# A recurrence in chunks of 32 tokens over all four batches instead of chunks of 64 over two, ahead of a mixture-of-experts attention and an MLP

## The chip, the core and the metric

One Trainium2 chip, one of its cores. The time is the device time in microseconds (us) of one launch. Three runs of the kernel before took 1216.72, 1219.43 and 1217.4 us, median 1217.4.

## What is computed

Three stages in float32. Batch B = 4, heads H = 8, sequence S = 768, head width D = 40. The first is a linear recurrence with a state of 40x40 for each batch and head:

```python
for t in range(S):
    y[:, :, t] = np.einsum('bhd,bhde->bhe', rt, state)
    Sa = np.einsum('bhde,bhe->bhd', state, at)
    state_decay = state * wt[:, :, None, :] - np.einsum('bhd,bhe->bhde', Sa, bt)
    state = state_decay + np.einsum('bhd,bhe->bhde', vt, kt)
```

Its output, 4x768x320, goes through causal attention with 4 experts (two are chosen for each token by a gate) and then through a gated MLP with a product over the sequence (768x768). The change touches the recurrence and what stands around it; attention and MLP keep their code.

## The kernel before

**The recurrence in chunks.** Within a chunk of tokens the recurrence becomes matrix products: a product with the state at the chunk's start, a triangular system that couples the chunk's tokens (its inverse is applied as a product), and the update of the state. The kernel before (`recurrence`, L55 to L509) has chunks of 64 tokens, two batches at a time, and goes through 24 steps (2 pairs of batches, 4 units of 3 chunks each).

**A step's chain** (`p2`). `f_w` (L370): right side of the system, from state and values. `f_u1` (L387): inverse of the first 32x32 block. `f_t21` (L397): the coupling of the two blocks. `f_u2` (L404): inverse of the second. `f_s` (L416): update of the state. Between two of them ScalarE copies PSUM to SBUF (L374, L391, L400), and after the last VectorE adds the old state and scales it (L419, L420). That makes five products one after the other. Between them the program puts the output of the step before (`rr`, `vt`, `amat`, `ys`, `yk`: L295, L302, L316, L333, L341) and, in `pump`, pieces of the preparation.

**The preparation** (`p1`, one unit at a time). Loads of w, b, k and a in pieces of 30 KB (L134) are transposed on TensorE (L141). VectorE forms cumulative products of w by scans (`p_w`, L159, L165) and scales the others (L171, L178). `p_t` (L189) makes the triangular blocks, masked into SBUF by L193. `p_l` (L217) turns them so that 96 blocks of 32x32 lie on 96 partitions, `p_sub` (L227, L229) inverts them by 31 pairs of VectorE instructions, and `p_xt` (L237) turns the inverses back; ScalarE copies each turn (L196, L197, L218, L241). There are 8 units.

**What sets the order.** TensorE's order is the program's (`manual_schedule`). The other engines' queues are ordered by the compiler's own timeline, so that VectorE's order is seen only in the program built.

**Around it.** While the last unit runs, `tail` already works on the attention of batch 0 in the gaps; the weights and the input of that attention are made ready before (`pre`: `attn_prep`, `first_x`). Afterwards `blend` interleaves four `attention(b)` (weight 58.0 each) with the preparation of the MLP (`rest`) and four `mlp(b)` (49.8 each).

Of the kernel before, what the change touches and what calls it, by code (L numbers as in the profile page):

```python
# [7 lines left out]
F32 = mybir.dt.float32  # L8
# [47 lines left out]
def recurrence(ctx, tc, r, k, v, w, a, b, ident, store_x, pre=None, tail=None):
    nc = tc.nc
    B, H, S, D = r.shape
    C = 64
    BQ = 2  # L60
    CQ = 3
    UC = BQ * CQ
    UT = UC * C
    NU = S // (CQ * C)
    NP = H // 2
    TS = 96
    SL = UT // TS
# [24 lines left out]
    WL = [home(i, 3).tile([128, H, UT], F32, name=f"WL{i}") for i in range(3)]
    KBT = [home(i, 3).tile([128, NP, UC, Q], F32, name=f"KBT{i}") for i in range(3)]
    XTD = cp.tile([128, 2, H, UC, 32], F32, name="XTD")
    XT = [XTD[:64, i] for i in range(2)]
    TD = XTD[64:96].rearrange("j x h c t -> j (x h c t)").rearrange("j (t g h c) -> j t g h c", t=32, g=2, h=H)
    T21 = [XTD[96:, i] for i in range(2)] + [ep.tile([128, H, UC, 32], F32, name="T21")[96:]]
    RT = [cp.tile([Q, NP, BQ * C], F32, name=f"RT{i}") for i in range(RTB)]
    PP = [home(i, PPB).tile([Q, NP, UC, C + 1], F32, name=f"PP{i}") for i in range(PPB)]
    PEN = [home(i, 3).tile([D, H, UC], F32, name=f"PEN{i}") for i in range(3)]  # L100
    W65 = [ap.tile([Q, UC * (C + 1) + 1], F32, name=f"W65{i}") for i in range(2)]
    RPE = [ap.tile([Q, UC, C + 1], F32, name=f"RPE{i}") for i in range(2)]
    ABD = [ap.tile([Q, UT], F32, name=f"ABD{i}") for i in range(2)]
    VU = [cp.tile([128, H, C], F32, name=f"VU{q}") for q in range(BQ)]
    SV = [[cp.tile([128, H, C], F32, name=f"SV{q}{i}") for i in range(2)] for q in range(BQ)]
    S0 = [[cp.tile([Q, NP, 64], F32, name=f"S0{q}{i}") for i in range(2)] for q in range(BQ)]
    HR = [slice(h * 64, h * 64 + D) for h in range(2)]

    nc.vector.memset(mask, 1.0)
    for h in range(2):  # L110
        nc.gpsimd.affine_select(mask[h * 64:(h + 1) * 64], mask[h * 64:(h + 1) * 64], pattern=[[1, C]],
                                compare_op=OP.is_gt, fill=0.0, base=0, channel_multiplier=-1)
    nc.vector.memset(scan1, 0.0)
    nc.vector.memset(scan1[:, :, 0:1], 1.0)
    for t in SLAB:
        nc.vector.memset(t[:, :, :, D:], 1.0)
    nc.vector.memset(RR[:, :, D:], 1.0)
    for t in W65:
        nc.vector.memset(t, 0.0)
    for t in WL + VU + sum(SV, []):  # L120
        nc.gpsimd.memset(t, 0.0)

    src = {"w": w, "k": k, "b": b, "a": a}
    uses = []

    def load(n):
        if n >= len(uses):
            return
        nm, i, p = uses[n]
        bb, u = units[i]  # L130
        for q in range(BQ):
            for z in range(SL // BQ):
                t0 = u * CQ * C + z * TS
                nc.sync.dma_start(SLAB[n % NSL][:, q * SL // BQ + z, :, :D],  # L134
                                  src[nm][bb * BQ + q, 2 * p:2 * p + 2, t0:t0 + TS, :].rearrange("h p d -> p h d"))

    def tr(nm, i, p):
        n = uses.index((nm, i, p))
        pt = ps.tile([128, SL, TS], F32, name="p1", bufs=P1B)
        for s in range(SL):  # L140
            nc.tensor.transpose(pt[:, s, :], SLAB[n % NSL][:, s].rearrange("p h d -> p (h d)"), ident[:TS, :TS])  # L141
        load(n + NSL)
        return pt[:Q].rearrange("e s p -> e (s p)")

    def ct(x):
        return x.rearrange("e (c t) -> e c t", c=UC)

# [1050 lines left out]
```

## Time and profile before

| | us |
|---|---|
| median of 3 runs | 1217.4 |
| span of the profiled execution (no other time is listed for it) | 1222.0 |
| TensorE busy / weight loads / VectorE / ScalarE / GpSimd | 1024.8 / 896.5 / 761.9 / 652.2 / 203.0 |
| first of the chain's products (L370) of the first step, last of the 24th | 100.1, 692.2 |
| last output product of the recurrence (L341) | 735.9 |

The profiled execution is 4.6 us (0.4%) above the median of the runs. Busy times of the engines overlap, so they are read by stretch and against what each waits for. In the trace a float32 matmul stands as two records (L370: 24 steps of 16 matmuls, 768 records); a transpose through TensorE is one record.

### The profile page before, as it was taken

To read this page: it belongs to the slowest core of one execution; us is meant where nothing else is said; L and a number is where in the kernel's file an instruction comes from. 1 tells how busy PE (TensorE), PEld (TensorE's weight loads), DVE (VectorE), ACT (ScalarE), POOL (GpSimd) and SP (SyncE) were. 2 spreads that over 40 slices of the span, in tenths; PEclk is the share of its full clock that TensorE was granted. 3 is DMA by queue.
4 is the path that set the end of the run, shared out by engine and by line. 5 is a ranking of instruction groups with operands and counts; after the bars stand their busy time and mean duration, and the time that the engine had idled before them with its cause. 6 is when DMAs were issued, how large, how long until landed. Compare 5 with 4: busy or idle time off the path is not lost.

```text
span 1222.0 us, 31926 instructions
## 1 busy us (share of the span) xinstructions
PE 1024.8 (84%) x12730; PEld 896.5 (73%) x12730; DVE 761.9 (62%) x1930; ACT 652.1 (53%) x1599; POOL 203.0 (17%) x381
## 2 busy tenths in 40 slices
PE   5757787787887969879797877798999899999998
PEld 3546676777776868768685665576898798789888
DVE  4586739467495474854835446988657656765650
ACT  2345564655645557465455445667555556555641
POOL 5011000010010100000002015802211211121131
PEclk9999767666766566676675766799999999989999
DMA  4333343333333333323211103210000001000000
GB/s 64 61 63 62 53 67 62 54 57 55 69 60 57 56 52 69 64 45 80 53 41 33 28 7 107 68 39 1 18 32 17 1 17 49 1 1 17 18 1 33
DMA packets 214663, 52.96 MB, mean 43 GB/s; under 512 B 204785, under 2 KB 210673, under 8 KB 214514
## 3 DMA queue, kind: packets, MB, share of 16 engines
q1 hardware_dynamic: 214514, 50.92, 21.2%
q8 instruction: 100, 1.64, 0.6%
q14 instruction: 49, 0.40, 0.1%
HBM read 39.07 MB, written 7.86 MB: 38 GB/s over the span
## 4 chain that ended last, share of the span: by engine, by line
PE 48%; DVE 28%; ACT 14%; issue 5%; DMA 3%; POOL 2%; SPq 1%; ACTq 0%; DVEq 0%; POOLq 0%
DVE X L229 5%; DVE sub L227 5%; PE mm L952 4%; PE mm L953 4%; PE mm L954 4%; ACT XTD L196 3%; ACT XTD L241 3%; PE p L141 2%; PE mp L911 2%; PE y L333 2%; PE mp L841 2%; PE pw L404 2%; PE y L341 2%; ACT f L881 2%; PE p L217 2%
## 5 line engine op out<-in xcount | busy, mean ns | idle before, releaser
L141 PE MATMUL p<-ident,slab 96*128 96x96 f32 x512 | 102.4, 340 | 43.7 <-ACT XTD L197 20.0
L141 PEld LDWEIGHTS p<-ident,slab 96*128 96x128 f32 x512 | 73.7, 194 | 60.7 <-ACT XTD L197 22.4
L227 DVE TENSOR_TENSOR sub<-L,X 96x31 f32<-96x31 f32 (+15 forms) x248 | 83.4, 336 | 17.0 <-ACT L L218 10.5
L196 ACT COPY XTD<-p 32x192 f32<-32x192 f32 x64 | 30.6, 479 | 110.4 <-DVE WL L193 109.9
L229 DVE TENSOR_TENSOR X<-X,sub 96x31 f32<-96x31 f32 (+15 forms) x248 | 83.1, 335 | 6.0
L881 ACT ACTIVATE f<-sc,nm 128x512 f32<-128x512 f32 (+2 forms) x110 | 59.4, 544 | 31.6 <-DVE nm L876 14.4
L602 DVE TENSOR_TENSOR ptl<-mp,pth 128x256 fp32r<-128x256 f32 (+2 forms) x126 | 57.0, 460 | 23.1 <-ACT pth L601 22.1
L876 DVE TENSOR_REDUCE nm<-sc 128x1 f32<-128x512 f32 (+2 forms) x110 | 54.6, 505 | 22.9 <-PE sc L874 18.6
L333 PE MATMUL y<-RT,S 40*40 40x64 f32 (+1 forms) x768 | 49.5, 308 | 22.4 <-DVE am L322 22.4
L159 DVE TENSOR_TENSOR_SCAN PP<-W,scan 104x390 f32<-104x390 f32 x32 | 30.9, 966 | 58.4 <-ACT W L157 58.4
L601 ACT CAST pth<-mp 128x256 fp32r<-128x256 f32 (+2 forms) x126 | 50.0, 409 | 32.3 <-PE mp L911 18.4
L202 POOL COPY PEN<-PP 40x6 f32<-40x6 f32 x64 | 25.7, 401 | 245.0 <-DVE PP L159 243.6
L333 PEld LDWEIGHTS y<-RT,S 40*40 40x40 f32 (+1 forms) x768 | 43.2, 194 | 25.6 <-DVE am L322 23.7
L193 DVE TENSOR_TENSOR WL<-p,mask 64x384 f32<-64x384 f32 x32 | 17.9, 560 | 67.6 <-PE xt L189 67.1
L316 PE MATMUL y<-RT,vut 40*64 40x64 f32 x1536 | 48.1, 259 | 12.2 <-ACT S L383 11.8
L911 PE MATMUL mp<-ident,f 128*128 128x128 f32 x294 | 51.5, 295 | 4.6 <-DVE f L897 2.3
L920 PE MATMUL pa<-pth,vv 128*128 128x256 f32 x168 | 47.5, 297 | 5.9 <-DVE at L932 3.8
L316 PEld LDWEIGHTS y<-RT,vut 40*64 40x64 f32 x1536 | 37.7, 164 | 19.0 <-ACT S L383 14.7
L952 PE MATMUL mm<-ws_h,vn_h 128*128 128x384 f32 x144 | 49.2, 341 | 0.4 <-ACT vn_h L601 0.3
L171 DVE TENSOR_TENSOR kb<-p,RPE 104x384 f32<-104x384 f32 x64 | 35.2, 554 | 22.4 <-PE p L141 20.9
L897 DVE TENSOR_SCALAR f<-f,sm 128x128 f32<-128x128 f32 (+2 forms) x96 | 45.3, 513 | 5.9 <-POOL sm L889 5.3
L953 PE MATMUL mm<-ws_l,vn_h 128*128 128x384 f32 x144 | 48.6, 338 | 0.0
(284 smaller groups left out, 3122.1 us busy)
## 6 DMA issues: line engine op xcount, KB each, us to landing
slab<-in_w_dram SPq DMA_DIRECT2D x128, 30.0 KB
slab<-in_b_dram SPq DMA_DIRECT2D x128, 30.0 KB
slab<-in_k_dram SPq DMA_DIRECT2D x128, 30.0 KB
slab<-in_a_dram SPq DMA_DIRECT2D x128, 30.0 KB
SV<-in_v_dram SPq DMA_DIRECT2D x48, 80.0 KB
VU<-in_v_dram SPq DMA_DIRECT2D x48, 80.0 KB
RR<-in_r_dram SPq DMA_DIRECT2D x48, 80.0 KB
WL<-ABD SPq DMA_DIRECT2D x64, 60.0 KB
```

Source lines behind the costliest of these rows:

```text
L141: nc.tensor.transpose(pt[:, s, :], SLAB[n % NSL][:, s].rearrange("p h d -> p (h d)"), ident[:TS, :TS])
L196: nc.scalar.copy(TD[:, :, g, n].rearrange("j t c -> j c t"), pt[gs, :, gs])
L227: nc.vector.tensor_mul(tv, L[:, j + 1:, j:j + 1].to_broadcast([96, n, m]), X[:, j:j + 1, :m].to_broadcast([96, n, m]))
L229: nc.vector.tensor_sub(X[:, j + 1:, :m], X[:, j + 1:, :m], tv)
L316: nc.tensor.matmul(pas[h][js, q, p], st["vut", q][HR[h], p, js], rt[q][HR[h], p], start=True, stop=True)
L333: nc.tensor.matmul(st["py"][q][hr.start:hr.start + m, p], s0[q][hr, p, :m], rt[q][hr, p], start=(p == 0), stop=False, skip_group_check=True)
L602: (lo_eng or nc.vector).tensor_sub(lo, src, hi.bitcast(F32))
L876: nc.vector.tensor_reduce(nm[:, z:z + 1], sc[:, :nn], op=OP.max, axis=AX.X, negate=True)
L881: nc.scalar.activation(pe[:, n0:n0 + nn], scs[z][:, :nn], AF.Exp, bias=nm[:, :1], accum_out=sm[:, z, i - i0:i - i0 + 1])
L911: nc.tensor.transpose(pp[:, j, z * 128:(z + 1) * 128], pes[z][:, (j0 + j) * 128:(j0 + j + 1) * 128], ident)
L952: nc.tensor.matmul(ps_, ah, bh, start=first, stop=False)
L953: nc.tensor.matmul(ps_, ah, bl_, start=False, stop=False)
```

## The change

The host lays w, k, b, a, r and v out anew (`layouts`): the 40 channels of a pair of batches on partitions 0 to 39 and 64 to 103, chunks of 32 tokens in 24 contiguous pieces of 104 rows. These loads and the transposes of L141 go; the 64x64 chunks become 32x32 and cover all four batches, batch q on partitions 32q to 32q+31. There is one 32x32 system to a chunk, so the chain is `f_w`, `f_u`, `f_s`. The triangular blocks of a unit (2, 2, 4, 4, 4, 4, 4 chunks, 32 blocks a chunk) go to DRAM and come back turned (`p_l`), are inverted by the same 31 pairs (`p_sub`), and go back the same way (`p_xt`). Twelve blocks of TensorE work make a step, each of 32 matmuls unless said: `f_lv` L235 (values' part of the right side), `f_w` L242, `f_u` L253, `f_kv` L264 (values' part of the update), `f_s` L272, `amat` L315, `ys` L332, `yk` L344, the transposes `f_st` L287 (the state, 8) and `vt` L297 (4), and for the preparation `p_t` L129 (64 for two chunks) and `p_x` L141 (8 transposes). PSUM tiles of `f_lv`, `f_w` and `f_u` fill one bank, one quadrant of rows to a batch. The attention of batch 0 no longer runs inside the recurrence's last unit: `first_x` and all of `attention(0)` follow it, and `wout_prep` moves behind `mlp_prep`.

```diff
@@ recurrence: the preparation
+SIZES = (2, 2, 4, 4, 4, 4, 4)
...
+    def p_w(s):
...
+        nc.vector.tensor_tensor_scan(PP[s].rearrange("e n t -> e (n t)"), w[:, :W - 1],
+                                     scan1.rearrange("e n t -> e (n t)"), 0.0, op0=OP.mult, op1=OP.add)
...
+        nc.vector.reciprocal(inj[:, :, C:], PP[s][:, :, C:])
...
+        nc.vector.tensor_tensor_scan(rp.rearrange("e n t -> e (n t)")[:, ::-1], w[:, 1:][:, ::-1],
+                                     inj.rearrange("e n t -> e (n t)")[:, ::-1], 0.0, op0=OP.mult, op1=OP.add)
...
+        nc.vector.tensor_mul(KB[s], xin[:, W:W + 2 * NW].rearrange("e (n j t) -> e n j t", n=NH, j=2),
+                             rp[:, :, None, 1:].to_broadcast([Q, NH, 2, C]))
...
+        nc.vector.tensor_mul(AT[s], xin[:, W + 2 * NW:].rearrange("e (n t) -> e n t", n=NH), PP[s][:, :, :C])
+        load(s + 3)
...
+    def p_t(s):
...
+        for j in range(2):
+            for h in range(H):
+                for q2 in range(2):
+                    for z in range(2):
+                        n = 2 * h + q2
+                        nc.tensor.matmul(pz[64 * q2:64 * q2 + 64, z, j, h],
+                                         KB[s + j][half(z), n].rearrange("e j t -> e (j t)"), AT[s + j][half(z), n],
+                                         start=(j == 0 and h == 0), stop=True, skip_group_check=True)
+        nc.vector.tensor_mul(LL[k][:, :, c * H:(c + 2) * H], pt.rearrange("p z (n t) -> p z n t", t=C),
+                             mask[:, None, None, :].to_broadcast([128, 2, 2 * H, C]))
...
+    def p_l(k):
...
+        for q in range(4):
+            nc.sync.dma_start(lo[q], LL[k][rows(q ^ 1), q % 2, :n])
+        for q in range(4):
+            nc.sync.dma_start(L[q * n:(q + 1) * n], lo[q].rearrange("j n t -> n j t"))
...
+    def p_sub(k, j0, j1):
...
+        for j in range(j0, j1):
+            n, m = C - 1 - j, j + 1
...
+            nc.vector.tensor_mul(tv, X[:, :m, j:j + 1].to_broadcast([m_, m, n]),
+                                 L[:, j:j + 1, j + 1:].to_broadcast([m_, m, n]))
+            nc.vector.tensor_sub(X[:, :m, j + 1:], X[:, :m, j + 1:], tv)
...
+    def p_xt(k):
...
+        nc.sync.dma_start(xo.rearrange("q n l t -> (q n) (l t)"), LX[k][1][:4 * n].rearrange("n l t -> n (l t)"))
+        for q in range(4):
+            nc.sync.dma_start(XT[k][rows(q), :n], xo[q].rearrange("n l t -> l n t"))
@@ recurrence: the chain and the output
+    def f_lv(g):
...
+        for h in range(H):
+            for q in QS:
+                nc.tensor.matmul(pw[g][rows(q), h], LL[k][rows(q), q % 2, c + h], V[g][rows(q), h], start=(h == 0),
+                                 stop=False, skip_group_check=True)
...
+    def f_w(g):
+        for h in range(H):
+            for q in QS:
+                n = 2 * h + q // 2
+                nc.tensor.matmul(pw[g][rows(q), h], AT[g][half(q % 2), n], ST[g % 2][half(q % 2), n, :D], start=False,
+                                 stop=True, skip_group_check=True)
+        wsb[g] = cp.tile([128, H, D], F32, name="wsb")
+        nc.scalar.copy(wsb[g], pw[g])
...
+    def f_u(g):
...
+        for h in range(H):
+            for q in QS:
+                nc.tensor.matmul(pu[rows(q ^ 1), h], XT[k][rows(q), c + h], wsb[g][rows(q), h], start=(h == 0), stop=True,
+                                 skip_group_check=True)
+        nc.scalar.copy(U[g % 2][:, :, :D], pu)
...
+    def f_s(g):
...
+        for h in range(H):
+            for q in QS:
+                z = q % 2
+                nc.tensor.matmul(pS[half(z), q // 2, h * D:(h + 1) * D], KBT[g][rows(q ^ 1), z, h],
+                                 U[g % 2][rows(q ^ 1), h, :D], start=False, stop=True, skip_group_check=True)
...
+        nc.vector.tensor_add(new,
+                             pS[:Q, :, :H * D].rearrange("e q (h d) -> e q h d", h=H),
+                             old)
...
+        nc.vector.tensor_mul(new, new, pe.to_broadcast([Q, 2, H, D]))
...
+    f_lv(0)
+    for g in range(NS):
+        last = g == NS - 1
+        f_w(g)
+        f_st(g)
+        amat(g - 1)
+        if not last:
+            f_kv(g)
+        run_until(3 * g + 1)
+        f_u(g)
+        ys(g - 1)
+        yk(g - 1)
+        load_rv(g + 1) if g else None
+        run_until(3 * g + 2)
+        if not last:
+            f_s(g)
+        load_v(g + 2)
+        vt(g)
+        f_lv(g + 1)
@@ kernel_body
-            recurrence(ctx, tc, r, k, v, w, a, b, ident, store_x, pre, tail)
-            parts["run"](None)
+            recurrence(ctx, tc, shape, x_in, rv_in, v_in, ident, store_x, pre)
+            with tc.tile_pool(name="staging", bufs=3, side="right") as st:
+                for _ in first_x(tc, xd, kx, st, xs):
+                    pass
...
-            blend([[parts["first"], CA, p0, 1.0]] + [[parts["attn"](b), 58.0, b, b + 1.0] for b in range(1, B)],
-                  [[rest(), RESTW, p0, 1.0 - lag]]
+            blend([[attention(b), 58.0, b, b + 1.0] for b in range(B)],
+                  [[rest(), RESTW, 0.0, 1.0 - lag]]
```

TensorE's order, from the output of one step to the chain's first product of the next. Before (`rr`, a slab's and a `kb`'s transposes, `yk`, then the 16 matmuls of `f_s`, of which two stand here):

```order
L295 MATMUL p_2868<-ident,RR 128x128 x4
L141 MATMUL p_2876<-ident,slab_88 128x96 x4
L206 MATMUL p_2896<-ident,kb 128x104 x3
L341 MATMUL y<-am,KBT_94 40x64 x16
L416 MATMUL pw<-VU_112,KBT_94 40x40
L416 MATMUL pw<-VU_113,KBT_94 40x40
```

In the kernel after (`yk`, `p_t`, `f_s`, `vt`, `f_lv`, `p_x`, and `f_w` of the next step):

```order
L344 MATMUL f<-am,kbt 40x32 x32
L129 MATMUL f<-at,kb 64x32 x64
L272 MATMUL ps<-U_95,kbt 40x40 x32
L297 MATMUL f<-ident,U_95 128x128 x4
L235 MATMUL pw<-v,ll 32x40 x32
L141 MATMUL f<-ident,kb 128x104 x8
L242 MATMUL pw<-ST_94,at 32x40 x32
```

Each line of the chain and of the output now stands for 32 matmuls of 32 or 40 columns, `p_t` lies between `yk` and `f_s`, and `vt`, `f_lv` and `p_x` lie between `f_s` and the next `f_w`.

VectorE's order around the state's update. Before (two batches' updates L419, L420 between the pairs of the inverse):

```order
L229 TENSOR_TENSOR X<-X,sub 96x14x18
L419 TENSOR_TENSOR SV_114<-pw,SV_115 40x8x40
L419 TENSOR_TENSOR SV_116<-pw,SV_117 40x8x40
L227 TENSOR_TENSOR sub<-L,X 96x247
L420 TENSOR_TENSOR SV_114<-SV_114,PEN_104 40x8x40
L420 TENSOR_TENSOR SV_116<-SV_116,PEN_104 40x8x40
L229 TENSOR_TENSOR X<-X,sub 96x13x19
L178 TENSOR_TENSOR ABD_111<-p_2586,PP_102 104x384
L227 TENSOR_TENSOR sub<-L,X 96x240
```

In the kernel after (step 5: output L348, all of `p_w` of a chunk, the update L276 and L280):

```order
L348 TENSOR_TENSOR xs<-f,pp 104x512
L102 SCALAR_TENSOR_TENSOR pp<-xin,scan_86 104x528
L105 RECIPROCAL INJ_90<-pp 104x16
L113 TENSOR_TENSOR at<-xin,pp 104x512
L107 SCALAR_TENSOR_TENSOR rp<-xin,INJ_90 104x528
L110 TENSOR_TENSOR kb<-xin,rp 104x1024
L276 TENSOR_TENSOR ST_93<-ps,ST_94 104x2x8x40
L280 TENSOR_TENSOR ST_93<-ST_93,pp 104x2x8x40
```

The five instructions of `p_w` now stand together behind the output's L348 and ahead of the update.

VectorE's order where an inverse begins. Before (unit 0; L171 and L178 belong to the unit after it):

```order
L171 TENSOR_TENSOR kb<-p_586,RPE_108 104x6x64
L227 TENSOR_TENSOR sub<-L,X 96x31
L171 TENSOR_TENSOR kb<-p_620,RPE_108 104x6x64
L229 TENSOR_TENSOR X<-X,sub 96x31
L178 TENSOR_TENSOR ABD_110<-p_636,PP_100 104x384
L227 TENSOR_TENSOR sub<-L,X 96x60
L229 TENSOR_TENSOR X<-X,sub 96x30x2
```

In the kernel after (end of step 6 and beginning of step 7, unit 4; `ll` is the last piece of that same unit):

```order
L110 TENSOR_TENSOR kb<-xin,rp 104x1024
L132 TENSOR_TENSOR ll<-f,mask 128x2x512
L276 TENSOR_TENSOR ST_94<-ps,ST_93 104x2x8x40
L280 TENSOR_TENSOR ST_94<-ST_94,pp 104x2x8x40
L168 TENSOR_TENSOR sub<-X,L 128x31
L170 TENSOR_TENSOR X<-X,sub 128x31
L168 TENSOR_TENSOR sub<-X,L 128x60
L170 TENSOR_TENSOR X<-X,sub 128x2x30
```

The pairs of the inverse now follow the unit's own last `ll` (L132) with only the update of the state between them, and run on as a block: 30 of 31 pairs stand ahead of the next update. The same stands in steps 3, 11 and 15.

What VectorE's list holds in each step besides its own four instructions (the masked output product L319, L348, L276, L280), counted from the built program; a step ends with its update of the state, and the first step is step 0:

| step | instructions of `p_w` (5 to a chunk) | of the inverse (62 to a unit) | L132 |
|---|---|---|---|
| 0 | 54 | 87 | 4 |
| 1 | 6 | 84 | 1 |
| 3 | 5 | 44 | 1 |
| 7, 11 (each) | 4 | 60 | 0 |
| 15 | 0 (16 of `attn_prep`) | 53 | 0 |
| 4, 6, 8, 10, 12 | 5 or 6 | 0, and 18 in step 4, 2 in steps 8 and 12 | 1 |
| 2, 5, 9, 13 | 4 or 5 | 0, and 15 in step 2 | 0 |
| 14 | 0 | 0 | 1 |
| 16 to 22 | 0 | 0, and 9 in step 16 | 0 |

## Rows read from the trace of the kernel before

**Rows 1.** The page: busy time of each engine; the chain that ended last, by engine.

```profile
PE 1024.8 (84%) x12730; PEld 896.5 (73%) x12730; DVE 761.9 (62%) x1930; ACT 652.1 (53%) x1599; POOL 203.0 (17%) x381
...
PE 48%; DVE 28%; ACT 14%; issue 5%; DMA 3%; POOL 2%; SPq 1%; ACTq 0%; DVEq 0%; POOLq 0%
```

**Rows 2.** Stretches of the span: length, busy time (x instructions) of each engine, granted clock, DMA.

```profile
core 0: us, PE busy (x) PEld busy (x) DVE busy (x) ACT busy (x) POOL busy (x), PEclk, DMA share, GB/s
0.00:100.00 100.00, 59.60 (x600) 44.12 (x600) 59.50 (x138) 38.39 (x85) 25.63 (x53) 1.00 0.38 63
100.00:628.00 528.00, 436.23 (x8421) 387.68 (x8422) 334.96 (x812) 291.44 (x664) 38.21 (x87) 0.68 0.33 59
628.00:737.00 109.00, 89.58 (x1091) 71.72 (x1087) 50.22 (x132) 53.48 (x140) 17.48 (x35) 0.67 0.11 25
737.00:816.00 79.00, 62.10 (x315) 49.41 (x314) 63.75 (x156) 49.63 (x134) 39.22 (x61) 0.78 0.28 82
816.00:1222.00 406.00, 377.24 (x2314) 343.60 (x2313) 253.50 (x693) 219.21 (x578) 82.48 (x147) 0.97 0.05 16
```

**Rows 3.** The source view of L370, the chain's first product: records, ns, first and last start.

```profile
L370 PE MATMUL pw<-SV,WL x768: 221/229/330, 100.1 to 692.2; 128*64 128x40 f32 x192
```

**Rows 4.** Timeline of TensorE within one step: start, length, what.

```profile
401.82 0.78 PE L206 MATMUL p<-ident,kb 104*128 104x104 f32 x3
...
404.39 1.90 PE L302 MATMUL y<-ident,VU 128*128 128x128 f32 x8
...
416.98 1.13 PE L316 MATMUL y<-RT,vut 40*64 40x64 f32 x32
...
419.51 1.28 PE L397 MATMUL pw<-wsb,XTD 32*32 32x40 f32 x32
```

**Rows 5.** Timeline of TensorE in the last step.

```profile
728.12 1.16 PE L316 MATMUL y<-RT,vut 40*64 40x64 f32 x64
```

**Rows 6.** Stretches around those of rows 4 and 5, for the clock.

```profile
728.10:729.30 1.20, 1.20 (x68) 1.12 (x66) 0.99 (x4) 1.10 (x4) 0.00 (x0) 1.00 0.06 14
...
419.50:420.80 1.30, 1.30 (x35) 1.20 (x36) 1.30 (x3) 0.00 (x0) 0.00 (x0) 0.50 0.44 67
```

**Rows 7.** VectorE in 100 to 640 us by shape: count, busy us, mean ns, idle before.

```profile
L322 DVE TENSOR_TENSOR am<-y,mask 128x512 f32<-128x512 f32 x42 | 27.0, 681 | 3.8 <-PE y L316 3.7
...
L344 DVE TENSOR_TENSOR xs<-y,PP 104x256 f32<-104x256 f32 x42 | 17.7, 421 | 23.2 <-PE y L341 21.7 <-DMA RR<-in_r_dram 1.3
...
L159 DVE TENSOR_TENSOR_SCAN PP<-W,scan 104x390 f32<-104x390 f32 x24 | 23.2, 965 | 40.5 <-ACT W L157 40.5
```

**Rows 8.** The page's groups of the inverse's pairs.

```profile
L227 DVE TENSOR_TENSOR sub<-L,X 96x31 f32<-96x31 f32 (+15 forms) x248 | 83.4, 336 | 17.0 <-ACT L L218 10.5
...
L229 DVE TENSOR_TENSOR X<-X,sub 96x31 f32<-96x31 f32 (+15 forms) x248 | 83.1, 335 | 6.0
```

**Rows 9.** Timeline of VectorE, an inverse's first pair.

```profile
416.56 0.20 DVE L227 TENSOR_TENSOR sub<-L,X 96x31 f32<-96x31 f32 x1 [0.90 <-ACT L L218]
...
416.80 0.21 DVE L229 TENSOR_TENSOR X<-X,sub 96x31 f32<-96x31 f32 x1
```

**Rows 10.** ScalarE in 100 to 640 us by shape.

```profile
L374 ACT COPY wsb<-pw 32x320 f32<-32x320 f32 x44 | 18.3, 417 | 23.0 <-PE pw L370 22.5
```

**Rows 11.** The page's DMA queue: packets, MB, share of 16 engines.

```profile
q1 hardware_dynamic: 214514, 50.92, 21.2%
```

**Rows 12.** Timeline of the DMA queue: four issues in a row.

```profile
413.98 1.79 SPq L134 DMA_DIRECT2D slab<-in_a_dram  x4
```

**Rows 13.** Timeline of a load of 3 KB and of its first reader.

```profile
746.41 0.24 SPq L675 DMA_DIRECT2D big<-in_moe_b_spatial_dram  x1
...
748.18 0.83 ACT L601 CAST bs<-big 1x768 fp32r<-1x768 f32 x1
```

**Rows 14.** Attention on TensorE in 628 to 737 us.

```profile
L869 PE MATMUL p<-kk,qq 128*128 128x512 f32 (+3 forms) x18 | 9.6, 535 | 4.1 <-ACT f L881 2.6 <-ACT qq L845 1.5
...
L920 PE MATMUL xt<-pth,vv 128*128 128x256 f32 (+1 forms) x18 | 8.5, 471 | 7.8 <-ACT pth L601 7.8
```

More of the change, by code (lines that the diff above doesn't have):

```diff
@@ L106, in recurrence @@
[L106 to L112 removed]
+    dp = ctx.enter_context(tc.tile_pool(name="rdram", bufs=1, space=DRAM))
+    sub_stack, prep_stack = ExitStack(), ExitStack()
@@ L113, in recurrence @@
+    scan1 = ap.tile([Q, NH, C + 1], F32, name="scan1")
     nc.vector.memset(scan1, 0.0)
     nc.vector.memset(scan1[:, :, 0:1], 1.0)
[L115 to L120, printed above, removed]
-        nc.gpsimd.memset(t, 0.0)
[L123 to L135, printed above, removed]
@@ L463, in run_until @@
+    when = sorted([x for k in range(len(SIZES)) for x in positions(k)], key=lambda x: x[0])
     def run_until(gap):
@@ L510, in recurrence @@
-    _, _, amat, ys, yk = outs[-1]
-    for f in (lambda: amat(0), lambda: amat(1), ys, yk):
-        f()
-    if tailq is not None:
-        tailq(TPC / 100)
+            x[1](*x[2:])
+    order = ctx.enter_context(tc.manual_schedule(engines={mybir.EngineType.PE}))
+    for s in range(3):
+        load(s)
+    load_v(0)
+    load_rv(0)
+    load_v(1)
+    load_rv(1)
+    run_until(0)
+    QS = range(4)
+    pw, wsb = {}, {}
+    aq = {}
+    def f_lv(g):
+        if g >= NS:
+            return
+        k = unit_of[g]
+        c = (g - starts[k]) * H
+        pw[g] = ps.tile([128, H, D], F32, name="pw")
+        for h in range(H):
+            for q in QS:
+                nc.tensor.matmul(pw[g][rows(q), h], LL[k][rows(q), q % 2, c + h], V[g][rows(q), h], start=(h == 0),
+                                 stop=False, skip_group_check=True)
@@ new lines, in recurrence @@
+    prep = None
+    f_lv(0)
[17 more added lines that the diff above has]
+        f_lv(g + 1)
+        run_until(3 * g + 3)
+        if not any(x[1] in (p_w, p_t, p_x) for x in when) and prep_stack is not None:
+            prep_stack.close()
+            prep_stack = None
+        if not when and sub_stack is not None:
+            sub_stack.close()
+            sub_stack = None
+            prep = pre() if pre is not None else None
+        for _ in range(PRQ):
+            if prep is not None:
+                next(prep, None)
@@ L517 @@
+    amat(NS - 1)
+    ys(NS - 1)
+    yk(NS - 1)
+    if prep is not None:
+        for _ in prep:
+            pass
 LEAST = 3.4332275390625e-05
```

693 lines of the change are left out of this document (247 added, 446 removed).

## The prediction, made before the changed kernel ran

> **What bounds the kernel now.** I read the page's busy times first, then the stretches, then the first product's rows, then single instructions. TensorE is busy for 84% of the span and makes 48% of the chain that ended last, VectorE 28% [rows 1]. Before 628 us TensorE's clock is granted to 0.68, after 816 us to 0.97 [rows 2]. The recurrence fills 100 to 737 us: L370 starts first at 100.1 and last at 692.2 us [rows 3], so a step takes 592.1 / 23 = 25.7 us. In 100 to 628 us TensorE is busy for 83% and VectorE for 63% [rows 2]: both fill a step, and neither waits long. The reader is to see that a chain shorter by two products is worth nothing unless the work falls too. So I cost the whole recurrence anew, step by step, and compare its end.
>
> **TensorE in a step.** Of today's blocks, 32 records take 1.28 us in the chain (two quadrants of columns in one quadrant of rows) and 1.13 us in `amat`; three transposes of 104 columns take 0.78 us and eight of 128 take 1.90 us [rows 4]. These are at or near the half clock of 1.2 GHz (0.50) [rows 6]. At the full 2.4 GHz 64 records of `amat` take 1.16 us [rows 5, 6], where twice 1.13 is 2.26.
>
> The change makes 32 matmuls, 64 records, of each chain block, spread on four quadrants. I charge 64 on four as 32 on two, 1.28 us, say 1.3. No row shows four quadrants of rows at once, so this has bounds: half of it if the clock is full, and twice if two run together and no more. `amat` stays at 2.0, `ys` and `yk` have half the columns on four pieces of the array, 1.5 each by `amat`'s rows, `f_st` 8 transposes, 1.6 with sharing of today's overlap, `p_t` 128 records, 3.6.
>
> On the path of every step: `f_w` 1.3, `f_st` 1.6, `amat` 2.0, `f_kv` 1.3, `f_u` 1.3, `ys` 1.5, `yk` 1.5, together 10.5 us. ScalarE's copies between them (L374 takes 0.42 us [rows 10]) lie beside other blocks and cost nothing; without that cover it would be some 0.8 us a step. Then `f_s` 1.3 and the update. `vt` and `f_lv` run beside the update.
>
> On VectorE 512 elements take 0.68 us and 256 take 0.42, thus 1.02 ns an element more; 390 elements of scan take 0.965 us [rows 7]. So an update's two instructions of 640 take 0.81 each, 1.6 us, L132's 1024 take 1.2, and `p_w` takes two scans of 528 (1.31 each), 1.2, 0.68 and 0.2: 4.7 us. A unit's inverse is 62 instructions at 0.336 [rows 8], 20.8 us.
>
> *Last steps (16 to 22):* 10.5 + 1.3 + 1.6 = 13.4 us at the half clock. At the full one 10.5 and 1.3 shrink by 1.16 / 2.0 = 0.58 to 6.9, sum 8.5. With today's share of full clock (0.68 is 36% of the time at full) 11.6.
>
> *Steps with `p_w` (2, 5, 9, 13):* the order shows `p_w` behind the output's L348 and ahead of the update. L348 waits for `yk`, so 0.7 + 4.7 us come after `yk`, and `f_s` hides under them: 10.5 + 5.4 + 1.6 = 17.5 at half, 13.1 at full; 16.
>
> *Steps with `p_t` as well (4, 6, 8, 10, 12):* `p_t` needs that `p_w`, and `f_s` stands behind `p_t` on TensorE: 3.6 + 1.3 more at half, 2.9 at full: 22.4 and 16.0; 20.
>
> *Heavy steps (3, 7, 11, 15):* the inverse is VectorE's block. Its list in these steps, by the instruction counts of the table, makes 25, 28, 28 and 31 us (the last with `attn_prep`). Ahead of it stands a wait: the unit's blocks go to DRAM and back first. Four issues take 1.8 us [rows 12]; a load lands and is read 1.8 us after its issue [rows 13]; 214514 packets used 21.2% of 16 engines' 1222 us, 19.3 ns each [rows 11], so the 4096 pieces of 128 bytes of a unit take 4096 x 19.3 / 16 = 4.9 us. 1.8 + 1.8 + 1.8 + 4.9 = 10.3 us, of which the update covers 1.6: 9 us of idle VectorE, and TensorE stalls with it, as the masked product for `yk` waits in the same list. I keep 4 and 12 as ends. 112 + 36 = 148 us.
>
> *Start and step 1:* VectorE's list up to the first update is 11 `p_w` (51.7), 87 instructions of inverses (29) and four L132 (4.8), 86 us; it begins at some 4 us, an estimate from a landing of 1.8 us [rows 13] behind an issue at about 1 us and a second load behind it. Step 1 has 41 us. Between dependent small instructions 0.04 us pass (416.56 + 0.20 to 416.80 [rows 9]); 434 of them make 17 us. 4 + 86 + 41 + 17 = 148 us.
>
> *Sum of the recurrence:* 148 + 148 + 5 x 20 + 4 x 16 + 15 (step 14) + 7 x 11.6 + 15 (step 23 and its output) = 571 us, against 737 today. The loads are 1.9 MB a step in long rows on a queue that is now shared by fewer, larger pieces; at today's 59 GB/s [rows 2] they would need 32 us a step and would bound it, but today's rate is one of pieces of 237 bytes in the mean (50.92 MB in 214514 [rows 11]) with the engines 67% idle. I cost them at nothing; if they come late the steps with `p_w` show it first.
>
> **What moves behind it.** Today part of batch 0's attention runs before 737 us: 18 of a batch's 32 records of L869 and 18 of 48 of L920 [rows 14], about 0.57 with the earlier products. The stretch from 816 us holds three attentions and four MLPs, 3 x 58 + 4 x 49.8 = 373 of `blend`'s units in 406 us [rows 2], 1.09 us a unit; so 0.57 x 58 x 1.09 = 36 us return. `first_x` now stands alone: a load behind the last store, three pieces split, 8 us. `wout_prep` costs nothing beside attention while GpSimd is at half (39 of 79 us, 737 to 816 us [rows 2]); uncovered, up to 14 us. Today 1222 - 737 = 485 us follow; 485 + 36 + 8 = 529.
>
> **Sum:** 571 + 529 = 1100 us on the trace's scale. The traced execution is 4.6 us above the runs' median; in that ratio, **1095 us**.
>
> **A rule weighed.** Rows 5 show 64 records, weight loads included, in 1.16 us at the full clock, under 17 ns from start to start. The Trainium skill, "TensorE: Matmul & The Clock Gate", Part 1, says that starts never come closer than about 25 ns however few the columns. By it the 448 records on a step's path would take at least 11.2 us at any clock, some 2.4 us more than mine in each of 17 light steps, and the sum would be near 1136. The trace speaks against the rule, so the sum goes by the row; 2 in 100.
>
> **Rivals.**
> - *The clock stays full and the turned blocks come early.* Denser work on four quadrants speaks for it, the stalls of the heavy steps against. Light steps at their full-clock ends: 5 x 16 + 4 x 13.1 + 7 x 8.5 + 23 = 215 for 275, and waits of 4 us: 20 less. **1015 us.** 20 in 100.
> - *Hand-offs.* VectorE's masked product L319 comes late as well, because the order was set by other durations than the chip's, and each of 17 light steps loses 4 us. **1163 us.** 13 in 100.
> - *Quadrants that share a bank take turns.* `f_lv`, `f_w` and `f_u` write four quadrants of rows into one PSUM bank. Rows 4 show two at a time with the same rows; alone a record costs 2 x 1.28 / 32 = 0.08 us at half, so 64 take 5.1 instead of 1.3. `f_w` and `f_u` lose 3.8 each, `f_kv` and `f_s`, two to a bank, 1 each: 9.6 us a step at half, 8 with the clock's share, 136 over 17 light steps. **1230 us, slower than before.** It decides from 122 / 17 = 7.2 us a step on. The Trainium skill states such a rule ("TensorEngine Tiling (Array Packing)", Restrictions and Gotchas: different row tiles cannot use one PSUM bank at the same time). No row here shows four rows at once; today's `amat`, whose row halves go to two banks, neither bears it out nor refutes it. 5 in 100.
> - *The chain is not what shrinks.* The path of a last step has 10.5 us of output and copies of the state in line with 3 products; if these, not the chain, set the step, the change does not do what it says, and yet the time is mine: that is the forecast.
>
> **How the numbers follow.** Forecast 60, full clock 20, hand-offs 13, shared bank 5, the page's floor 2. The range: low ends together (light steps 215 for 275, waits of 4 us, and 17 us of moved attention taken up by TensorE's idle 79 - 62 us of the stretch from 737 [rows 2]) give 998; high ends (light steps 311, waits of 12 us, `wout_prep` uncovered and twice the 8 us of `first_x`) 1165. Both are moved out by some 10 us for the start, which has no bounds of its own: 985 to 1175. It leaves out the shared bank and the tails of two others, under 2 in 10. About 0.2% is what a measurement of this kernel can tell from no change (its runs lie 0.22% apart). Faster 94, the same 1, slower 5 in 100.
>
> **What would show it.** First update at about 100 us, second near 145; L242 starts in steps 16 to 22 some 11 to 12 us apart; VectorE idle before the first L168 of steps 3, 7, 11 and 15 for about 9 us, ended by the load of L; steps 4, 6, 8, 10, 12 longer than 5 and 9 by some 4; last L348 near 570 us; from there to the end about 529. Wrong would be: L253 and L242 with 64 records in over 2.5 us at half clock (shared bank), or a chain that ends in DMA.

## The result, and the profile after

The changed kernel takes **1198.57 us** (median of 4 runs, 1195.38 to 1206.05), the kernel before 1218.41 beside it: ratio 0.985, interval 0.9815 to 0.9884. The interval lies clear of 1, so it is faster, but by 1.5% only, a sixth of what was forecast, and the time lies above the upper end of the range. The profiled execution spans 1193.3 us, 0.4% under its median.

The page of the kernel after: busy times, the DMA queues, the chain by engine.

```profile
PE 899.8 (75%) x17018; PEld 805.7 (68%) x17018; DVE 698.4 (59%) x1645; ACT 379.7 (32%) x1095; POOL 151.4 (13%) x278
...
q1 hardware_dynamic: 108298, 77.01, 27.8%
q8 instruction: 133, 2.18, 0.8%
...
PE 51%; DVE 27%; DMA 10%; issue 6%; ACT 4%; SPq 1%; POOL 1%; DVEq 0%; ACTq 0%; POOLq 0%
```

Against [rows 1] TensorE has a third more instructions (17018 for 12730) in 125 us less busy time: it idles more. Share of issue in the chain rises from 5 to 6%, of DMA from 3 to 10%.

Stretches of the kernel after, cut at updates of the state (L276) and at the end of the last L348 (columns as in [rows 2]): to the first update, step 1, step 3, step 14, steps 17 to 22, step 23 with its output, and all that follows. The clock's 1.00 in the first three is no reading (see the last section).

```profile
0.00:110.04 110.04, 39.67 (x972) 35.28 (x972) 78.78 (x148) 10.69 (x41) 8.30 (x22) 1.00 0.63 141
110.04:150.72 40.68, 21.80 (x668) 19.61 (x668) 38.08 (x96) 4.13 (x16) 1.11 (x2) 1.00 0.36 83
...
169.78:211.72 41.94, 22.58 (x705) 20.46 (x705) 23.69 (x56) 4.13 (x16) 0.00 (x0) 1.00 0.39 80
...
456.52:481.21 24.69, 18.24 (x612) 17.02 (x613) 4.26 (x7) 2.60 (x10) 0.00 (x0) 0.50 0.25 52
...
532.64:630.49 97.85, 85.70 (x3145) 77.30 (x3146) 18.20 (x24) 14.21 (x48) 0.00 (x0) 0.53 0.34 73
630.49:652.70 22.21, 17.13 (x592) 15.45 (x592) 4.41 (x6) 3.01 (x10) 0.00 (x0) 0.50 0.22 42
652.70:1193.30 540.60, 479.93 (x2842) 427.08 (x2842) 363.78 (x966) 300.65 (x806) 137.01 (x242) 0.93 0.09 28
```

The recurrence ends at 652.7 us (forecast 571, before 737) and 540.6 us follow (529, before 485). By steps, measured against forecast: start and step 1 150.7 to 148; the four heavy steps 151.8 to 148; steps 4, 6, 8, 10, 12 109.6 to 100; steps 2, 5, 9, 13 80.2 to 64; step 14 24.7 to 15; steps 16 to 22 113.5 to 81; step 23 with its output 22.2 to 15. On the trace's scale the miss is 93 us (1193.3 for 1100): 82 inside the recurrence and 12 behind it. Of the 82 us, 68 lie in the 17 light steps, 32 of these in the seven (16 to 22) that have no preparation on TensorE, and 7 in step 23 with its output.

What TensorE waited for in the kernel after, 70 to 653 us (waited for: us, times, longest):

```profile
PE pw L242 <- DVE ST L280: 34.1, 8, 12.2
...
PE f L344 <- DVE am L319: 23.6, 4, 8.1
PE pw L235 <- issue: 15.0, 7, 4.1
...
PE f L129 <- issue: 14.2, 8, 3.7
```

The waits for VectorE are few and long, in the start, in the heavy steps and right behind them. New are the waits for "issue", in which no engine and no transfer is waited for: 66.8 us in 49 places over all lines, where the kernel before had 2.3 us in three. One of them in TensorE's timeline of a last step, in the middle of a product whose operands are all there (columns as in [rows 4]; in brackets the idle time before, and its releaser):

```profile
566.23 1.29 PE L235 MATMUL pw<-v,ll 32*32 32x40 f32 x64
567.45 0.74 PE L242 MATMUL pw<-ST,at 40*32 40x40 f32 x27
570.65 0.88 PE L242 MATMUL pw<-ST,at 40*32 40x40 f32 x37 [2.46 <-issue]
571.46 1.65 PE L287 MATMUL f<-ident,ST 104*128 104x104 f32 x8
```

### The profile page after: what moved, and what is told of

It is laid out like the page before. It is cut to its first block, busy times and chain, and to the rows that moved or that the text cites. A ratio compares the mean times of both kernels' runs of the same rounds, so it can differ in the third digit from the quotient of the medians.

```text
span 1193.3 us, 38319 instructions
## 1 busy us (share of the span) xinstructions
PE 899.8 (75%) x17018; PEld 805.7 (68%) x17018; DVE 698.4 (59%) x1645; ACT 379.7 (32%) x1095; POOL 151.4 (13%) x278
## 3 DMA queue, kind: packets, MB, share of 16 engines
q8 instruction: 133, 2.18, 0.8%
## 4 chain that ended last, share of the span: by engine, by line
PE 51%; DVE 27%; DMA 10%; issue 6%; ACT 4%; SPq 1%; POOL 1%; DVEq 0%; ACTq 0%; POOLq 0%
DVE sub L168 5%; DVE X L170 5%; DMA xin<-in_x_dram 5%; PE mm L827 5%; PE mm L828 4%; PE mm L829 4%; PE f L332 3%; PE f L315 3%; PE mp L786 3%; PE ps L264 3%; PE mp L716 2%; PE f L287 2%; PE pu L253 2%; PE f L344 2%; PE pw L242 2%
## 5 line engine op out<-in xcount | busy, mean ns | idle before, releaser
L141 PE MATMUL f<-ident,kb 104*128 104x104 f32 x192 | 38.0, 373 | 84.1 <-DVE ll L132 42.7
L168 DVE TENSOR_TENSOR sub<-X,L 128x31 f32<-128x31 f32 (+28 forms) x217 | 73.3, 338 | 44.1 <-DMA L<-lo 37.9
L141 PEld LDWEIGHTS f<-ident,kb 104*128 104x128 f32 x192 | 30.4, 213 | 87.0 <-DVE ll L132 43.6
L348 DVE TENSOR_TENSOR xs<-f,pp 104x512 f32<-104x512 f32 x24 | 16.6, 690 | 113.1 <-PE f L344 113.1
L756 ACT ACTIVATE f<-sc,nm 128x512 f32<-128x512 f32 (+3 forms) x128 | 68.9, 543 | 36.2 <-DVE nm L751 17.6
L170 DVE TENSOR_TENSOR X<-X,sub 128x31 f32<-128x31 f32 (+28 forms) x217 | 73.2, 337 | 6.2
L751 DVE TENSOR_REDUCE nm<-sc 128x1 f32<-128x512 f32 (+3 forms) x128 | 63.0, 502 | 23.4 <-PE sc L749 20.3
L319 DVE TENSOR_TENSOR am<-f,mask 128x512 f32<-128x512 f32 x24 | 16.5, 689 | 99.6 <-PE f L315 99.6
L242 PE MATMUL pw<-ST,at 40*32 40x40 f32 x1536 | 30.3, 254 | 41.0 <-DVE ST L280 34.1
L129 PE MATMUL f<-at,kb 40*64 40x32 f32 x1536 | 47.4, 292 | 17.2 <-issue 14.2
L129 PEld LDWEIGHTS f<-at,kb 40*64 40x64 f32 x1536 | 45.1, 221 | 19.2 <-issue 15.8
L344 PE MATMUL f<-am,kbt 64*40 64x32 f32 x1536 | 36.9, 253 | 27.2 <-DVE am L319 23.6
L242 PEld LDWEIGHTS pw<-ST,at 40*32 40x32 f32 x1536 | 26.0, 154 | 46.1 <-DVE ST L280 36.1
L797 PE MATMUL pa<-ptl,vv 128*64 128x256 f32 x192 | 52.3, 294 | 2.2 <-DVE ptl L477 1.6
L344 PEld LDWEIGHTS f<-am,kbt 64*40 64x40 f32 x1536 | 32.9, 170 | 28.7 <-DVE am L319 24.1
L786 PEld LDWEIGHTS mp<-ident,f 128*128 128x128 f32 x336 | 43.8, 154 | 12.3 <-DVE f L772 4.1
```

The costliest lines, as they stand in the source:

```text
L129: nc.tensor.matmul(pz[64 * q2:64 * q2 + 64, z, j, h], KB[s + j][half(z), n].rearrange("e j t -> e (j t)"), AT[s + j][half(z), n], start=(j ...
L141: nc.tensor.transpose(pt[:, h // 4, h % 4 * Q:(h % 4 + 1) * Q], kb[:, h], ident[:Q, :Q])
L168: nc.vector.tensor_mul(tv, X[:, :m, j:j + 1].to_broadcast([m_, m, n]), L[:, j:j + 1, j + 1:].to_broadcast([m_, m, n]))
L170: nc.vector.tensor_sub(X[:, :m, j + 1:], X[:, :m, j + 1:], tv)
L242: nc.tensor.matmul(pw[g][rows(q), h], AT[g][half(q % 2), n], ST[g % 2][half(q % 2), n, :D], start=False, stop=True, skip_group_check=True)
L344: nc.tensor.matmul(py[half(z), q2, c:c + C], KBT[g][64 * q2:64 * q2 + 64, z, 2 * p + h], am[64 * q2:64 * q2 + 64, h, z * HP + p], start=Fa ...
```

## The experiments

Four theories stood. **S**: TensorE's instructions come in pieces of 16 KB (q8 moved 2.18 MB in 133 packets; 17018 records and as many weight loads are 256 a packet), each piece takes some 3.5 us to come, and a light step needs 4.1 of them. **C**: the products' own time at the half clock sets the light steps. **D**: the data loads delay the pieces. **O**: VectorE's order, which holds an inverse in one block, makes the heavy steps; its rival **H** is that a fixed order only moves the waits.

**More instructions** (`e1_tiny`), in `amat`:

```diff
+        for x in range(128):
+            q, o = x % 4, 448 + x // 4 % 32 * 2
+            nc.tensor.matmul(pa[rows(q), q % 2, o:o + 2], mask[rows(q), :32], mask[rows(q), :2], start=False, stop=True,
+                             skip_group_check=True)
```

> The changed kernel with 128 more matmuls of 2 columns in each step (256 records, 512 instructions of TensorE with the weight loads; two in each quadrant of rows at a time, into columns that nothing reads). Theory S (the supply of TensorE's instructions sets the light steps: one 16-KB piece holds 256 instructions, and a piece takes at least 3.5 us): steps 16 to 22 go from 16.2 us in the mean to 23 to 24.5, the last L348 from 652.7 us to 775 or later. Theory C (the products' own time at the half clock sets them): 256 records at the 16.6 ns that this kernel's records show there are 4.2 us, steps 16 to 22 become 20.4 us, and the last L348 ends near 740.

Measured: 1358.75 us; steps 16 to 22 took 23.8 us each, the last L348 ended at 818.7. S, not C: 7.6 us a step for 512 instructions. The page counts 48 packets more:

```profile
q8 instruction: 181, 2.97, 0.9%
```

24 steps x 512 instructions in 48 packets make 256 instructions a packet, that is 128 records with their 128 weight loads.

**The supply alone** (`e8_alone`), ahead of the recurrence:

```diff
+    dense = ident.bitcast(BF16)
+    pa = ps.tile([128, 2, 512], F32, name="f", bufs=FBQ)
+    for x in range(48):
+        nc.tensor.matmul(pa[:, 0, :256], dense[:, :128], dense[:, :256], start=x == 0, stop=True, skip_group_check=True)
+    for x in range(1024):
+        q, o = x % 4, x // 4 % 8 * 32
+        nc.tensor.matmul(pa[32 * q:32 * q + 32, 1, o:o + 32], mask[32 * q:32 * q + 32, :32], mask[32 * q:32 * q + 32, :32],
+                         start=o == 0, stop=True, skip_group_check=True)
```

> The changed kernel with 48 bf16 matmuls of 256 columns and then 1024 float32 matmuls of 32 columns on the four quadrants of rows ahead of the recurrence, where TensorE has nothing to do and few loads run: 2048 records, 4096 instructions with the weight loads, 16 pieces of 16 KB, with no other engine to wait for. Theory S: one piece every 3.3 to 3.8 us whatever the clock, so the 1024 matmuls take 53 to 61 us, 26 to 30 ns a record, in bursts with gaps every 256 instructions. Theory C: 9.5 ns a record at the full clock or 16.6 at the half one, 20 to 34 us without gaps. A floor on each start (25 ns from start to start) would give 51 us too, but evenly, with no burst at 9.5 to 17 ns.

TensorE's timeline of this run (L219 are the 48, L222 the 1024; the first rows), and below it the stretch of ten pieces:

```profile
10.76 1.67 PE L222 MATMUL f<-mask 32*32 32x32 f32 x175
19.72 1.93 PE L222 MATMUL f<-mask 32*32 32x32 f32 x128 [7.29 <-issue]
28.39 1.93 PE L222 MATMUL f<-mask 32*32 32x32 f32 x128 [6.73 <-issue]
36.23 1.93 PE L222 MATMUL f<-mask 32*32 32x32 f32 x128 [5.91 <-issue]
39.96 1.93 PE L222 MATMUL f<-mask 32*32 32x32 f32 x128 [1.80 <-issue]
```

```profile
41.64:77.56 35.92, 19.29 (x1299) 17.98 (x1289) 0.00 (x0) 0.00 (x0) 0.00 (x0) 0.50 0.02 5
```

These lines show the supply by itself. With nothing to wait for, TensorE does 128 records in 1.93 us, 13.3 ns from start to start (without the last record's own 0.24), and then stands still until the next piece is there. Ten pieces took 35.92 us, **3.59 us a piece or 28.1 ns a record**, at 5 GB/s of other traffic. S's figure holds, C's 16.6 ns and an even floor of 25 ns do not. The first three pieces, while the first chunks are loaded (171 GB/s in 10 to 37 us), took 8 to 9 us, which is what D says. The whole run took 1252.99 us.

**A higher clock** (`e6_dense`): 8 times 256 columns at three places of a step, in columns that nothing reads.

```diff
+    def more(out, first=False):
+        for x in range(8):
+            nc.tensor.matmul(out, dense[:, :128], dense[:, :256], start=first and x == 0, stop=True,
+                             skip_group_check=True)
...
+        more(pt[:, 1, :256], True)
...
```

> The changed kernel with 24 more bf16 matmuls of 256 columns in each step (48 instructions; into columns that nothing reads), to raise TensorE's granted clock in the recurrence without many instructions: 24 x 256 columns are 2.6 us at 2.4 GHz and 5.1 us at 1.2. Theory C (products at the half clock set the light steps): if the clock of 300 to 600 us goes from 0.56 to 0.9 or more, the products shrink by 0.58, and steps 16 to 22 take 8.5 + 2.6 = 11 to 13 us. Theory S (supply of instructions): whatever the clock, 572 instruction pairs are 4.3 pieces of 16 KB a step, at 3.5 us or more, so the steps stay at 15 us or more and within 2 us of today's 16.2. If the clock stays near 0.56 the run tells nothing of C except that 5.1 us more of array time would make 21 us by C and 16 to 18 by S.

Measured: 1210.35 us, granted clock 0.80 in steps 16 to 22, 16.8 us a step. The mean clock, 0.70 in 300 to 600 us, stayed under C's condition of 0.9, but single steps met it, and step 22 ran wholly at the full clock. Stretches of step 20 and step 22:

```profile
596.51:611.46 14.95, 13.39 (x549) 11.27 (x550) 3.03 (x4) 2.37 (x8) 0.00 (x0) 0.87 0.36 75
627.65:642.80 15.15, 12.13 (x549) 10.32 (x550) 3.03 (x4) 2.37 (x8) 0.00 (x0) 1.00 0.33 72
```

TensorE's timeline of step 22 (L248 is `f_w`, L293 `f_st`, L322 `amat`, L229 the added ones, L270 `f_kv`, L259 `f_u`, L340 `ys`, L353 `yk`):

```profile
630.78 0.33 PE L241 MATMUL pw<-v,ll 32*32 32x40 f32 x12 [1.11 <-issue]
631.05 0.79 PE L248 MATMUL pw<-ST,at 40*32 40x40 f32 x64
631.77 0.93 PE L293 MATMUL f<-ident,ST 104*128 104x104 f32 x8
632.63 0.89 PE L322 MATMUL f<-rv 40*64 40x32 f32 x43
634.37 0.54 PE L322 MATMUL f<-rv 40*64 40x32 f32 x21 [0.85 <-issue]
634.85 1.05 PE L229 MATMUL f<-ident 128*128 128x256 bf16 x8
635.82 1.13 PE L270 MATMUL ps<-v,kbt 32*64 32x40 f32 x64
636.89 0.54 PE L259 MATMUL pu<-wsb,xt 32*32 32x40 f32 x35
637.84 0.48 PE L259 MATMUL pu<-wsb,xt 32*32 32x40 f32 x29 [0.42 <-issue]
638.25 1.13 PE L340 MATMUL f<-rv,s 40*64 40x32 f32 x64
639.31 1.05 PE L229 MATMUL f<-ident 128*128 128x256 bf16 x8
640.29 0.49 PE L353 MATMUL f<-am,kbt 64*40 64x32 f32 x27
641.41 0.57 PE L353 MATMUL f<-am,kbt 64*40 64x32 f32 x37 [0.64 <-issue]
```

Between two waits lie 21 + 8 + 64 + 35 = 128 records, and 29 + 64 + 8 + 27 = 128 again; work resumes at 630.78, 634.37, 637.84 and 641.41 us, 3.47 to 3.59 apart, although the products run 1.6 times as fast (`f_w` 0.79 us where it took 1.29). C's 11 to 13 us are out of reach: the pieces set this step. At the half clock the two bounds lie close together: the blocks of a last step add up to 14.4 us in the kernel after, its 4.1 pieces to 14.7. So a higher clock would buy next to nothing. The four runs of the kernel after agree: at mean clocks of 0.798, 0.818, 0.831 and 0.855 they took 1199.42, 1195.38, 1197.72 and 1206.05 us.

**Fewer loads** (`e2_noload`): r and v are loaded for the first two steps alone, and later steps compute with these.

```diff
-        if g < NS:
+        if 2 <= g < NS:
+            RV[g] = RV[g % 2]
+        elif g < NS:
...
```

> The changed kernel without the loads of r and v after the first two steps: later steps use the first two steps' values (so its output is computed from other data). It tells whether the pieces of instructions arrive late because they share the DMA engines with these loads. Theory S: TensorE's waits for issue inside a product remain at 60 us or more of 70 to 653 us (66.8 now), steps 16 to 22 stay within 0.7 us of 16.2 in the mean. Theory D (data traffic delays the pieces): these waits fall below 25 us, and steps 16 to 22 fall to 14.5 us or less.

Measured: 1169.97 us; waits for issue 31.2 us instead of 66.8; steps 16 to 22 take 14.8 us for 16.2. Neither expectation holds whole: half of these waits was D. The 14.8 us fit the supply with little traffic, 4.1 x 3.59 = 14.7 us a step; as the products' 14.4 lie as near, this run does not tell S from C.

**VectorE in the program's order** (`e5_dve`):

```diff
-    order = ctx.enter_context(tc.manual_schedule(engines={mybir.EngineType.PE}))
+    order = ctx.enter_context(tc.manual_schedule(engines={mybir.EngineType.PE, mybir.EngineType.DVE}))
```

> The changed kernel with VectorE too in the program's order, as TensorE is: the inverse's pairs then lie 5 to 10 to a step in all steps from 2 to 19, no step has 30 of them, and its own four instructions of a step stand where the program puts them. Theory O (the order of VectorE makes the four heavy steps): steps 3, 7, 11 and 15 fall from 38 us in the mean to 17 to 21, the others change by under 2 us, the last L348 ends at 560 to 590 us and the kernel takes 1100 to 1145 us. Theory H (hand-offs: an order fixed by hand makes the update and the masked product wait behind pairs): each of 20 steps gains 2 to 4 us, which gives the saving back; 1170 us or more.

Measured: 1138.73 us, ratio to before 0.9324 (0.9281 to 0.9366). The heavy steps take 86.4 us together instead of 151.8, the start and step 1 12 us less; the other 17 steps to the last update grew by 26 us together. The recurrence ends at 600.7, later than expected by 11 us, the kernel within the range. O holds in the main: the heavy steps now take 21.6 us in the mean, where 17 to 21 was expected. That no other step would change by 2 us did not hold (step 12 grew by 6.3, steps 16 to 22 by 1.5 each), and H holds for that part.

**Preparation's products later** (`e7_late_pt`), on top of `e5_dve`, in `positions`; the round through DRAM (`l`) also starts earlier:

```diff
-            l, sub, xt = 3 * (g - 4.2), (3 * (g - 4.0), 3 * (g - 0.7)), 3 * (g - 0.6)
+            l, sub, xt = 3 * (g - 4.9), (3 * (g - 4.0), 3 * (g - 0.7)), 3 * (g - 0.6)
...
-                out.append((at[c] + 0.3, p_t, s - 1))
-            out.append((at[c] + 0.6 + (c + 1) % 2 * 0.05, p_x, s))
+                out.append((at[c] + (1.3 if k > 2 else 0.3), p_t, s - 1))
+            out.append((at[c] + (1.6 if k > 2 else 0.6) + (c + 1) % 2 * 0.05, p_x, s))
```

> The version with VectorE in program order, and in it the preparation's products moved: p_t and p_x of units 3 to 6 one gap later (p_t then lies behind f_lv, where TensorE waits for the update, and no longer between yk and f_s behind a p_w that is just starting), and the round through DRAM of units 4 to 6 0.7 step earlier. The version without this lost 33.8 us in p_t's waits for the scaled a and 12.5 us in p_x's. If the order of the work is what is left there (theory O), steps 4 to 13 go from 23 us in the mean to 18 to 20 and the kernel from 1138.7 to 1090 to 1110 us; the floor of theory S for these steps is 4.7 pieces of 16 KB x 3.5 = 16.3 us. If VectorE's own list (15 us in such a step) with its waits is the bound, under 10 us are gained.

Measured: 1138.61 us: nothing gained, though the wait it aimed at went (in the profiled executions the recurrence ended 6.5 us earlier). TensorE's waits in the recurrence, of `e5_dve` and of `e7_late_pt`:

```profile
PE f L129 <- DVE at L113: 33.8, 9, 5.2
PE pw L235 <- issue: 18.9, 7, 4.6
PE pw L242 <- DVE ST L280: 17.7, 9, 9.1
```

```profile
PE pw L242 <- DVE ST L280: 37.0, 12, 9.6
PE pw L235 <- issue: 24.2, 9, 4.5
...
PE f L129 <- DVE at L113: 5.2, 3, 2.2
```

28.6 us left L129; 19.3 came back at the chain's first product, as a wait for VectorE's update (L280), and 5.3 at L235 as issue. By its own expectation (under 10 us gained) VectorE's list with its waits bounds these steps more than TensorE's order does; how much of it the supply of instructions holds back is not shown.

**Fewer instructions** (`e9_merge`), on top of `e7_late_pt`: `f_kv` goes, and `f_s` contracts values and solution at once. For that ScalarE makes four more copies a step, and v is loaded in four pieces.

```diff
...
+            for q in QS:
+                nc.scalar.copy(V[g][rows(q ^ 1), q % 2], pu[rows(q ^ 1)])
...
+                r = slice(q // 2 * 64, q // 2 * 64 + 64)
+                nc.tensor.matmul(pS[half(z, n), q // 2, h * D:(h + 1) * D], flat[r, o:o + n], V[g][r, z, h],
+                                 start=(h == 0), stop=True, skip_group_check=True)
...
-        if not last:
-            f_kv(g)
```

> The version with VectorE in program order and p_t moved, with fewer TensorE instructions: the values' part of the state's update (f_kv) and the inverse's part (f_s) become one product. ScalarE writes the solution beside the values (four more copies of 32x320 in a step), so that one matmul contracts 64 rows where two had 32 each; V is loaded in four pieces. A step has 64 records, 128 instructions, half a piece of 16 KB fewer. Theory S (3.6 us a piece, as the 2048 records alone took): every step from 2 on gains 1.8 us, steps 16 to 22 go from 17.4 to 15.6, the kernel from 1138.6 to 1095 to 1105 us. If another wait sets these steps (the update behind pairs of the inverse, the copies on ScalarE), under 15 us are gained.

Measured: **1098.98 us, ratio to before 0.9018** (0.8954 to 0.9083), 39.6 us less than without the merge; the recurrence ends at 551.1 us, for 594.2. This is the fastest version of the study and beats both kernels. It does not tell S from C, as `f_kv` also took 1.94 us of array time at the half clock; `e1_tiny`, `e8_alone` and `e6_dense` do that. Steps 16 to 22 take 16.5 us where 15.6 was expected, though they have 460 records, 3.6 pieces. The stretches of these steps in `e2_noload`, in the kernel after and in `e9_merge`:

```profile
502.99:606.48 103.49, 92.88 (x3601) 84.19 (x3602) 23.18 (x38) 15.98 (x54) 0.00 (x0) 0.58 0.13 24
517.00:630.49 113.49, 98.15 (x3601) 88.89 (x3602) 23.15 (x38) 15.93 (x54) 0.00 (x0) 0.53 0.36 79
416.10:531.76 115.66, 90.94 (x3221) 82.12 (x3222) 45.65 (x104) 28.23 (x84) 0.65 (x2) 0.56 0.49 99
```

128 records took 3.68 us at 24 GB/s of traffic, 4.03 at 79 and 4.60 at 99, beside 3.59 at 5 GB/s in `e8_alone`. So the shorter steps of `e9_merge` lost to D a part of what they saved; TensorE waited there 21.5 us for issue and 2.9 for anything else.

## Why the prediction was wrong

**Right.** The direction; the start and step 1 (150.7 for 148); the heavy steps (151.8 for 148). Both sums owe something to luck: the first update came at 110.0 where about 100 was said, and step 1 took 40.7 where the sum has some 45; step 3 took 41.9 for 34, step 15 35.8 for 40. VectorE's idle time ahead of the first pair, costed at 9 us, was 37.9 us over the four:

```profile
L168 DVE TENSOR_TENSOR sub<-X,L 128x31 f32<-128x31 f32 (+28 forms) x217 | 73.3, 338 | 44.1 <-DMA L<-lo 37.9
```

**The step that failed** is "I charge 64 on four as 32 on two, 1.28 us", taken into the light steps as a price that falls with the clock, "with today's share of full clock (0.68 is 36% of the time at full) 11.6". One block did cost that: L235, L242 and L253 take 1.29 us for 64 records at the half clock and 0.79 at the full one. But blocks in a row cannot keep it up. 524 records, which is a last step, need 4.1 pieces, 14.7 us at either clock and 16.2 with the loads beside them. Over the seven last steps that is 32 of the 82 us. The clock was forecast too high as well (0.53 in steps 17 to 22, not 0.68), and `f_kv` takes 1.94 and `ys` 1.93 us instead of 1.3 and 1.5; by these alone the step would have come to 14 us or so, by coincidence near the supply's bound. So the supply alone accounts for the 4.6 us that a last step missed, but the slower products alone would have cost over half of them; that the supply holds when the products are fast is shown by steps 20 and 22 of `e6_dense`. Whether the clock would have risen without the waits for issue is not shown.

**Steps with `p_w`.** The 392 records up to `yk`, priced at 10.5 us at half and less at full, come at 28.1 ns, 11.0 us; with 5.4 + 1.6 behind them that is 18.0 for the 16 given. Measured were 20.1; the other 2 us are not settled. **Steps with `p_t`** were short by 1.9 us each (21.9 for 20). **Step 14** was a slip: the table of VectorE's list shows one L132 in it, so it has a `p_t` too, and I charged none; its 612 records are 4.8 pieces, 17.2 us, and without the loads of r and v it took 17.9 of the 24.7. The loads, costed "at nothing", so cost some 28 us for r and v alone (652.7 to 624.9), not by coming late themselves (TensorE waited for neither r nor v) but mostly, by the halved waits for issue, through the instructions that came late beside them. The output of step 23 missed by 7 us.

**Behind the recurrence** 540.6 for 529. `first_x` stayed under its price of 8 us: 5.4 from the last L348 to the first L682. In the chain of 645 to 690 us, however, VectorE's conversions of L457 to L460 (`wout_prep`, taken as free) make some 20%; that these are the missing 12 us is argued from the chain, not tried.

**The rivals.** Quadrants that share a bank do not take turns: 64 records in 1.29 us, not 5.1. The Trainium skill's rule ("TensorEngine Tiling (Array Packing)", Restrictions and Gotchas) does not show here. The floor of 25 ns that the Trainium skill states ("TensorE: Matmul & The Clock Gate", Part 1), given 2 in 100, does not hold here for each start (13.3 ns in `e8_alone`); the mean over more than 128 records, 28.1 ns, lies near it as a number, but it is made of bursts and gaps. I dismissed it by rows 5, a burst of 64 records, which fits into one piece and can't show this. The rule that did bear was one I had not used: the Trainium skill, "Runtime: NRT & Kernel Launch", Instruction fetch mechanics, says that instructions are refilled in blocks of 16 KiB, 256 instructions, and that crossing one is mostly hidden. The size agrees with the 48 packets of `e1_tiny`; hidden it was in the kernel before (2.3 us of issue; there 128 records took 8.0 us, by 8421 in 528 us [rows 2]), and is not here. The full clock did not come, and would have given little. Hand-offs were those of the heavy steps, as costed: TensorE's 23.6 us of waiting for L319 lie in these four. The 17 light steps did lose 4.0 us each, just what the rival of hand-offs gave them, but they lost it elsewhere.

## What to carry to other kernels

Price many small matmuls by the instructions they need as well as by a burst: here 128 records with their weight loads came every 3.6 us in the mean without traffic (two packets never closer than 3.28) and more slowly beside loads, and neither clock changed that, while fewer and deeper matmuls gave 40 us (by the supply and by shorter products, which that run does not part). A burst shorter than one piece can't show this bound; look for waits of "issue" inside a product, evenly spaced in instructions. And where a long block on one engine stops the others, spread it: the inverse's pairs laid over most steps gave 60 us.

## What was not expected of the hardware

- Instructions were not fetched further ahead while TensorE ran: packets of q8 that carry them lay never closer than 3.28 us in any run and took 1.1 us each. In `e8_alone` without loads a packet began some 1.1 us after TensorE had taken up the piece before, and TensorE went on some 2.5 us after the packet's start.
- Beside data traffic of 171 GB/s a piece took 8 or 9 us instead of 3.6. The packets themselves took 1.2 to 1.4 us there; it was their start that came later, twice 5 to 6 us after TensorE had taken up the piece before.
- Four quadrants of rows run at once into one bank at 13.3 ns a record at the half clock and 8.5 ns at the full (the first 175 records of `e8_alone`).
- The granted clock reads 1.00 until its first recorded change (254 us in the kernel after), while products there already take the times of the half clock (L242 1.29 us); such a reading is checked against a product's duration.
